# Joining the weights' sign bit on VectorE instead of ScalarE, and pooling the first keys on VectorE alone

## The chip, the core and the metric

The kernel runs on one core of a Trainium2 chip. The metric is device time in microseconds for one execution; the time before is the median of three runs. A profile of one further execution goes with it.

## What is computed

The program is pooled attention followed by a gated feed-forward layer, in float32 accuracy. There are 8 batches, 8 heads, 576 positions and a head size of 64, so 4608 tokens of width 512; the feed-forward layer is 1536 wide.

```python
k_p = k.reshape(B, H, Sp, 8, D).mean(axis=3)     # 72 pooled keys per batch and head
v_p = v.reshape(B, H, Sp, 8, D).mean(axis=3)
scores = scale * np.matmul(q, k_p.transpose(0, 1, 3, 2))
scores = scores - np.max(scores, axis=-1, keepdims=True)
attn = np.exp(scores)
attn = attn / (np.sum(attn, axis=-1, keepdims=True) + 1e-09)
x = np.matmul(attn, v_p)                         # then tokens x 512
g = x @ w_gate
silu = g * (1.0 / (1.0 + np.exp(-g)))
out = (silu * (x @ w_val)) @ w_out
```

The three weight matrices arrive as 64-bit floats. The kernel reads them as pairs of 32-bit words, a low and a high one, and builds a 32-bit float from each pair by integer operations and scaling.

## The kernel before

**Stages.** The 4608 tokens are cut into nine tiles of 512 columns. For each tile, attention makes x in chunks of at most 128 columns, and the feed-forward layer then runs over 12 weight blocks of 128 hidden columns. For accuracy nearly every operand is held as a high and a low part: x as xh and xl, the weights as wgv_h, wgv_l, wo_h and wo_l, the hidden activations as hh and hl. A block therefore needs 24 gate and value products (L423 to L425) and 12 output products (L407 to L409). The gate and value sums have one PSUM bank each; between the two groups of products stand a tanh (L427, ScalarE), two VectorE operations (L428, L431), a copy hh (L437, ScalarE) and a difference hl (L438, VectorE).

**The weights.** They stay in SBUF for the whole kernel and are converted once, while the first tile runs. Function `load_w` does one block of 128 x 1536 pairs: a load `ws` of 1.5 MB (L138); a shift of the low words by 29 (L141, VectorE); a write of the sign into the upper 16 bits of each low word (L143, ScalarE, a float16 output of the high word times 2^-60, of which only the sign remains); wf, the high word scaled without its sign (L146, ScalarE); the joining of wf and the low word (L148, VectorE). After that come the two maxima of the block (L155, ScalarE, each with a small read of its accumulator), the sum over partitions on TensorE and the power of two that scales the block (`pow2_above`, L126 to L133), the high parts (L168, ScalarE), the low parts (L169, VectorE), wo_h (L174, ScalarE) and wo_l (L175, GpSimd). Raw blocks share a pool of two buffers, `raw`; at the start one of the two holds the keys of batch 0. wf has one of three buffers of a pool `mid`, shared with keys, values and outputs.

**Keys and values.** `prep_k` loads a batch's keys in two halves (L199) and sums each group of 8 with `pool8`: on VectorE that is one reduction (L180), on GpSimd three additions of halves (L185 to L187). Before, VectorE does the first half of batch 0, and GpSimd everything else. Values go through the same three GpSimd additions, and then through a number of VectorE operations that split them (vst_h, vst_l, vst_f).

**A chunk of attention.** Eight small score products (L265), maxima and differences (L272, L273), an exponential (L281), sums and normalisation (L283 to L289), the weights as float16 halves (L295 and L297 on ScalarE, L298 and L299 on GpSimd), a transposing transfer issued by SyncE (L300), 16 products with the values (L309 to L312), then xh (L314, ScalarE) and xl (L315, VectorE).

**Order.** All engines work in order. The program is written as generators: before the first feed-forward step two chunks of attention are done, then each step takes four pieces of weight work (until the 12 blocks are done), one block of the feed-forward layer and three pieces of attention. The first tile runs its first three blocks in two halves of 256 columns. The framework then draws up each engine's order from estimated times and adds the waits, so the order of two independent instructions in the profile need not be that of the program.

Of the kernel before, what the change touches and what calls it, by code (L numbers as in the profile page):

```python
# [8 lines left out]
F16 = mybir.dt.float16  # L9
F32 = mybir.dt.float32  # L10
F32R = mybir.dt.float32r
U32 = mybir.dt.uint32
AF = mybir.ActivationFunctionType
ALU = mybir.AluOpType
# [30 lines left out]
def attention_then_swiglu(  # L45
# [9 lines left out]
    nc = tc.nc  # L55
# [3 lines left out]
    SP = S // POOLW  # L59
# [34 lines left out]
    for i in range(4):  # L94
# [3 lines left out]
        out=mask, in_=eye.rearrange("p (h k) -> p h k", h=4), axis=AX.X, op=ALU.add  # L98
# [23 lines left out]
    def pow2_above(dst, inv, src):  # L122

        ps = bank()
        sums = ps[:, : src.shape[1]]
        nc.tensor.matmul(sums, ones, src, start=True, stop=True)  # L126
        nc.vector.tensor_scalar(
            out=dst, in0=sums, scalar1=1e-30, scalar2=1.0 / UNIT, op0=ALU.max, op1=ALU.mult
        )
        nc.vector.tensor_single_scalar(  # L130
            dst.bitcast(U32), dst.bitcast(U32), 0x7F800000, ALU.bitwise_and
        )
        nc.vector.reciprocal(inv, dst)  # L133

    def load_w(c):

        ws = raw.tile([P, 3 * DM, 2], U32, name="ws", tag="raw")
        nc.sync.dma_start(out=ws, in_=w3[c].bitcast(U32))  # L138
        low, high = ws[:, :, 0], ws[:, :, 1]
        wf = mid.tile([P, 3 * DM], F32, name="wf", tag="mid")  # L140
        nc.vector.tensor_single_scalar(low, low, 29, ALU.logical_shift_right)  # L141

        nc.scalar.activation(  # L143
            ws.bitcast(F16)[:, :, 1], high.bitcast(F32), AF.Copy, scale=2.0**-60
        )
        nc.scalar.activation(wf, high.bitcast(F32), AF.Abs, scale=2.0**-112)  # L146
        yield
        nc.vector.scalar_tensor_tensor(  # L148
            out=wf.bitcast(U32), in0=wf.bitcast(U32), scalar=3, in1=low,
            op0=ALU.logical_shift_left, op1=ALU.bitwise_or,  # L150
        )
        wm = small.tile([P, 2], F32, name="wm")
        for i in range(2):
            part = wf[:, i * DM : (i + 1) * DM]
            nc.scalar.activation(  # L155
                wgv_h[:, c, i].rearrange("p j f -> p (j f)"), part, AF.Abs,
                accum_out=wm[:, i : i + 1],
            )
        yield
        sw = small.tile([P, 2], F32, name="sw")  # L160
        pow2_above(p2w[:, c, 0:2], sw, wm)
        nc.vector.tensor_mul(p2w[:, c, 2:3], p2w[:, c, 0:1], p2w[:, c, 1:2])
        yield
        for i in range(2):
            part = wf[:, i * DM : (i + 1) * DM]
            hi = wgv_h[:, c, i].rearrange("p j f -> p (j f)")
            lo = wgv_l[:, c, i].rearrange("p j f -> p (j f)")
            nc.scalar.activation(hi, part, AF.Copy, scale=sw[:, i : i + 1])  # L168
            nc.vector.scalar_tensor_tensor(  # L169
                out=lo, in0=part, scalar=sw[:, i : i + 1], in1=hi,  # L170
                op0=ALU.mult, op1=ALU.subtract
            )
        part = wf[:, 2 * DM :]
        nc.scalar.copy(wo_h[:, c, :], part)  # L174
        nc.gpsimd.tensor_sub(wo_l[:, c, :], part, wo_h[:, c, :].bitcast(F32))  # L175

    def pool8(eng, src, dst, inner):

        if eng is nc.vector:
            nc.vector.tensor_reduce(  # L180
                out=dst, in_=src.rearrange("p j (t i) -> p j i t", t=POOLW), axis=AX.X, op=ALU.add
            )
            return
        a, b4 = src[:, :, : 4 * inner], src[:, :, 4 * inner :]
        eng.tensor_add(a, a, b4)  # L185
        eng.tensor_add(a[:, :, : 2 * inner], a[:, :, : 2 * inner], a[:, :, 2 * inner :])
        eng.tensor_add(dst, a[:, :, :inner], a[:, :, inner : 2 * inner])  # L187

    def prep_k(b):
        ks = ksum[b % 2]  # L190
        for g in range(2):
            js = slice(g * NJ // 2, (g + 1) * NJ // 2)
            if b:
                kr = mid.tile([P, NJ // 2, S], F32, name="kr", tag="mid")
            else:
                if g == 0:
                    first = raw.tile([P, NJ, S], F32, name="k0", tag="raw")
                kr = first[:, js]
            nc.sync.dma_start(out=kr, in_=k[b, :, js])  # L199
            pool8(nc.gpsimd if b or g else nc.vector, kr, ks[:, js], SP)  # L200
            yield

    def prep_v(b):
# [118 lines left out]
    def prep(b):  # L322
        if b < B and b not in prepped:
            prepped.add(b)
            yield from prep_k(b)
            if b == 0:
                load_q(0, 0, SUB)
            yield from prep_v(b)
            yield
# [132 lines left out]
    def weights():  # L462
        for c in range(NCH):
            yield from load_w(c)
            ready.add(c)
# [112 lines left out]
```

## Time and profile before

| | |
|---|---|
| median of three runs | 1053.33 us (1053.12 to 1055.92) |
| the profiled execution | 1050.82 us, of which the span of the profile is 1049.0 us |
| TensorE busy | 991.8 us, 95% of the span |
| VectorE busy | 517.3 us, 49% |
| ScalarE busy | 332.7 us, 32% |
| GpSimd busy | 194.3 us, 19% |
| mean granted clock of TensorE | 0.993 |

The busy shares are averages over stages that differ: the weights are converted in the first fifth of the span, and the remaining tiles only use them. The rows below therefore go by stretches of time, counted from the start of the span. In them PE is TensorE, DVE VectorE, ACT ScalarE, POOL GpSimd and SPq SyncE's queue of transfers. A line number such as L143 is that of the kernel file.

### The profile page before, as it was taken

To read this page: it belongs to the slowest core of one execution; us is meant where nothing else is said; L and a number is where in the kernel's file an instruction comes from. 1 tells how busy PE (TensorE), PEld (TensorE's weight loads), DVE (VectorE), ACT (ScalarE), POOL (GpSimd) and SP (SyncE) were. 2 spreads that over 40 slices of the span, in tenths; PEclk is the share of its full clock that TensorE was granted. 3 is DMA by queue.
4 is the path that set the end of the run, shared out by engine and by line. 5 is a ranking of instruction groups with operands and counts; after the bars stand their busy time and mean duration, and the time that the engine had idled before them with its cause. 6 is when DMAs were issued, how large, how long until landed. Compare 5 with 4: busy or idle time off the path is not lost.

```text
span 1049.0 us, 13336 instructions
## 1 busy us (share of the span) xinstructions
PE 991.8 (95%) x5320; PEld 602.2 (57%) x5320; DVE 517.3 (49%) x1013; ACT 332.7 (32%) x549; POOL 194.3 (19%) x223
## 2 busy tenths in 40 slices
PE   3378989999999999999999999999999999999998
PEld 2256556665556655665566555655665556555555
DVE  6586878754246543644256435542553245223222
ACT  3897874332123312221133113311332132212111
POOL 5226136520006100610062005200110011000000
PEclk9998999999999999999999999999999999999999
DMA  7655435430032202410051006100210021001001
GB/s 283 203 178 185 155 90 151 159 67 13 1 111 80 52 1 73 129 31 1 35 161 41 7 5 187 46 1 0 77 40 16 1 75 27 1 1 41 1 1 41
DMA packets 81214, 72.43 MB, mean 69 GB/s; under 512 B 53504, under 2 KB 69888, under 8 KB 79616
## 3 DMA queue, kind: packets, MB, share of 16 engines
q1 hardware_dynamic: 81152, 71.58, 22.4%
q8 instruction: 42, 0.69, 0.3%
q14 instruction: 20, 0.16, 0.1%
HBM read 50.33 MB, written 9.44 MB: 57 GB/s over the span
## 4 chain that ended last, share of the span: by engine, by line
PE 84%; DVE 6%; ACT 4%; issue 3%; DMA 2%; POOL 1%; SPq 0%; ACTq 0%; POOLq 0%
PE gv L423 17%; PE gv L425 16%; PE gv L424 16%; PE acc L407 9%; PE acc L408 9%; PE acc L409 9%; PE ps L265 5%; ACT ws L143 2%; DVE wgv_l L169 1%; DVE wf L148 1%; PE ps L309 1%; DMA vr<-v_main 1%; DMA ws<-w_all 1%; PE ps L312 1%; PE ps L310 1%
## 5 line engine op out<-in xcount | busy, mean ns | idle before, releaser
L423 PE MATMUL gv<-xh,wgv_h 128*128 128x512 f16 (+1 forms) x888 | 334.6, 377 | 4.9 <-ACT xh L314 3.0
L425 PE MATMUL gv<-xh,wgv_l 128*128 128x512 f16 (+1 forms) x888 | 333.1, 376 | 1.5 <-DVE wgv_l L169 1.5
L424 PE MATMUL gv<-xl,wgv_h 128*128 128x512 f16 (+1 forms) x888 | 333.6, 376 | 0.0
L428 DVE SCALAR_TENSOR_TENSOR hf<-hf,gv 128x512 f32<-128x512 f32 (+1 forms) x111 | 74.3, 670 | 256.9 <-ACT hf L427 256.9
L407 PE MATMUL acc<-hh,wo_h 128*128 128x512 f32 (+1 forms) x444 | 184.0, 433 | 2.5 <-ACT hh L437 2.5
L408 PE MATMUL acc<-hl,wo_h 128*128 128x512 f32 (+1 forms) x444 | 172.5, 390 | 0.1
L409 PE MATMUL acc<-hh,wo_l 128*128 128x512 f32 (+1 forms) x444 | 171.8, 389 | 0.0
L427 ACT ACTIVATE hf<-gv,un 128x512 f32<-128x512 f32 (+1 forms) x111 | 74.7, 673 | 290.1 <-PE gv L425 290.1
L423 PEld LDWEIGHTS <-wgv_h 128*128 128x128 f16 x888 | 88.0, 99 | 110.5 <-issue 18.7
L425 PEld LDWEIGHTS <-wgv_l 128*128 128x128 f16 x888 | 87.6, 99 | 100.3 <-DVE wgv_l L169 1.8
L424 PEld LDWEIGHTS <-wgv_h 128*128 128x128 f16 x888 | 88.0, 99 | 86.2 <-issue 1.1
L437 ACT CAST hh<-hf 128x512 fp32r<-128x512 f32 (+1 forms) x111 | 67.6, 609 | 204.0 <-DVE hf L431 203.9
L431 DVE SCALAR_TENSOR_TENSOR hf<-gv,un,hf 128x512 f32<-128x512 f32 (+1 forms) x111 | 81.4, 734 | 82.6 <-PE gv L425 81.8
L298 POOL TENSOR_TENSOR half<-sc,half 128x512 f16<-128x512 f32 (+1 forms) x40 | 49.6, 1241 | 324.4 <-issue 244.7
L438 DVE TENSOR_TENSOR hl<-hf,hh 128x512 fp32r<-128x512 f32 (+1 forms) x111 | 81.0, 730 | 51.0 <-ACT hh L437 50.5
L407 PEld LDWEIGHTS acc<-hh,wo_h 128*128 128x128 f32 x444 | 82.5, 188 | 27.6 <-ACT hh L437 3.1
L409 PEld LDWEIGHTS acc<-hh,wo_l 128*128 128x128 f32 x444 | 83.8, 189 | 17.9
L408 PEld LDWEIGHTS acc<-hl,wo_h 128*128 128x128 f32 x444 | 84.1, 189 | 17.0 <-DVE hl L438 0.3
L265 PE MATMUL ps<-ksum,qt 64*128 64x72 f32 (+1 forms) x640 | 76.1, 286 | 11.8 <-DMA qt<-q_rows 8.9
L265 PEld LDWEIGHTS ps<-ksum,qt 64*128 64x128 f32 (+1 forms) x640 | 63.6, 190 | 38.6 <-issue 20.3
L185 POOL TENSOR_TENSOR kr<-kr 128x576 f32<-128x576 f32 x14 | 22.5, 1607 | 295.5 <-DMA kr<-k_rows 230.3
L309 PE MATMUL ps<-pt,vst_h 128*128 128x128 f16 (+1 forms) x160 | 33.8, 222 | 18.9 <-DMA pt<-half 18.0
(89 smaller groups left out, 833.8 us busy)
## 6 DMA issues: line engine op xcount, KB each, us to landing
ws<-w_all SPq DMA_DIRECT2D x12, 1536.0 KB, 6.9
out_t<-ob SPq DMA_DIRECT2D x36, 256.0 KB, 2.2
qt<-q_rows SPq DMA_DIRECT2D x32, 256.0 KB, 3.2
vr<-v_main SPq DMA_DIRECT2D x16, 512.0 KB, 3.9
kr<-k_rows SPq DMA_DIRECT2D x14, 576.0 KB, 4.4
vr<-v_left SPq DMA_DIRECT2D x8, 512.0 KB, 3.7
k<-k_rows SPq DMA_DIRECT2D x2, 576.0 KB, 4.3
qt<-q_rows SPq DMA_DIRECT2D x8, 128.0 KB, 2.6
```

The source lines that it names most:

```text
L265: nc.tensor.matmul(pss[g][:n, j * SP : (j + 1) * SP], qt[rows, j, :n], ksum[b % 2][rows, j, :], start=True, stop=True,)
L407: nc.tensor.matmul(o, wo_h[:, c, js], hh[:, :n], start=begin, stop=False)
L408: nc.tensor.matmul(o, wo_h[:, c, js], hl[:, :n], start=False, stop=False)
L409: nc.tensor.matmul(o, wo_l[:, c, js], hh[:, :n], start=False, stop=end)
L423: nc.tensor.matmul(o, wh, xh[:, j, a:e], start=(j == 0), stop=False)
L424: nc.tensor.matmul(o, wh, xl[:, j, a:e], start=False, stop=False)
L425: nc.tensor.matmul(o, wl, xh[:, j, a:e], start=False, stop=(j == NJ - 1))
L427: nc.scalar.activation(hf[:, :n], pss[0], AF.Tanh, scale=un[:, c, 0:1])
L428: nc.vector.scalar_tensor_tensor(out=hf[:, :n], in0=hf[:, :n], scalar=1.0, in1=pss[0], op0=ALU.add, op1=ALU.mult)
L431: nc.vector.scalar_tensor_tensor(out=hf[:, :n], in0=pss[1], scalar=un[:, c, 2:3], in1=hf[:, :n], op0=ALU.mult, op1=ALU.mult,)
L437: nc.scalar.copy(hh[:, :n], hf[:, :n])
L438: nc.vector.tensor_sub(hl[:, :n], hf[:, :n], hh[:, :n].bitcast(F32))
```

## The change

The ScalarE write of the sign is replaced by a VectorE operation that takes the sign bit from the high words and joins it to the low words, in 32-bit words and in place. It stands between the shift and the scaling in the program. In `prep_k`, both halves of batch 0's keys go to VectorE; later batches stay on GpSimd.

```diff
         nc.vector.tensor_single_scalar(low, low, 29, ALU.logical_shift_right)
-
-        nc.scalar.activation(
-            ws.bitcast(F16)[:, :, 1], high.bitcast(F32), AF.Copy, scale=2.0**-60
+        nc.vector.scalar_tensor_tensor(
+            out=low, in0=high, scalar=0x80000000, in1=low, op0=ALU.bitwise_and, op1=ALU.bitwise_or
         )
         nc.scalar.activation(wf, high.bitcast(F32), AF.Abs, scale=2.0**-112)
...
             nc.sync.dma_start(out=kr, in_=k[b, :, js])
-            pool8(nc.gpsimd if b or g else nc.vector, kr, ks[:, js], SP)
+            pool8(nc.gpsimd if b else nc.vector, kr, ks[:, js], SP)
```

## Rows read from the trace of the kernel before

**Rows 1.** Busy time by stretch; x is instructions, PEclk the mean granted clock.

```profile
core 0: us, PE busy (x) PEld busy (x) DVE busy (x) ACT busy (x) POOL busy (x), PEclk, DMA share, GB/s
20.00:55.00 35.00, 11.59 (x66) 9.37 (x66) 22.12 (x53) 30.79 (x32) 8.62 (x7) 1.00 0.55 171
55.00:120.00 65.00, 54.02 (x362) 39.49 (x361) 51.45 (x105) 53.06 (x76) 27.44 (x25) 0.92 0.60 207
...
58.00:70.00 12.00, 8.98 (x69) 7.47 (x67) 10.77 (x24) 10.68 (x23) 4.21 (x5) 0.86 0.84 280
...
120.00:190.00 70.00, 65.03 (x385) 40.04 (x384) 55.14 (x106) 43.36 (x73) 27.92 (x28) 0.98 0.33 94
20.00:190.00 170.00, 130.64 (x810) 88.90 (x810) 128.71 (x263) 127.21 (x179) 63.98 (x60) 0.96 0.48 153
190.00:1049.00 859.00, 854.13 (x4471) 507.56 (x4470) 375.95 (x723) 202.23 (x366) 116.61 (x137) 1.00 0.16 46
```

**Rows 2.** Waits up to 55 us: total us, times, longest us.

```profile
PE ps L309 <- DMA pt<-half: 11.4, 2, 9.7
PE ps L126 <- DVE xl L315: 3.2, 1, 3.2
...
DVE wf L148 <- ACT ws L143: 6.6, 3, 5.0
```

**Rows 3.** TensorE's waits from 55 to 190 us, same columns.

```profile
PE ps L309 <- DMA pt<-half: 6.6, 3, 3.5
PE gv L423 <- ACT xh L314: 3.0, 1, 3.0
PE acc L407 <- ACT hh L437: 2.5, 2, 2.0
...
PE gv L423 <- DVE hf L431: 0.4, 1, 0.4
```

**Rows 4.** Instructions of single lines: ns min/median/max, first and last start.

```profile
L143 ACT ACTIVATE ws<-ws x12: 3581/3637/3699, 21.6 to 143.6; 128x1536 f16<-128x1536 f32 x12
...
L146 ACT ACTIVATE wf<-ws x12: 1576/1618/1699, 19.5 to 147.5; 128x1536 f32<-128x1536 f32 x12
...
L141 DVE TENSOR_SCALAR ws<-ws x12: 944/950/1252, 20.1 to 142.5; 128x1536 uint32<-128x1536 uint32 x12
...
L148 DVE SCALAR_TENSOR_TENSOR wf<-wf,ws x12: 1741/1758/2089, 25.2 to 149.4; 128x1536 uint32<-128x1536 uint32 x12
...
L180 DVE TENSOR_REDUCE ksum<-k x1: 2218/2218/2218, 5.8 to 5.8; 128x144 f32<-128x1152 f32 x1
```

**Rows 5.** Timeline of ScalarE, three places: start us, us, instruction.

```profile
28.77 3.62 ACT L143 ACTIVATE ws<-ws 128x1536 f16<-128x1536 f32 x1
...
32.14 0.67 ACT L295 CAST half<-sc 128x512 f16<-128x512 f32 x1
...
44.60 3.60 ACT L143 ACTIVATE ws<-ws 128x1536 f16<-128x1536 f32 x1
47.96 0.67 ACT L314 ACTIVATE xh<-ps,r 128x512 f16<-128x512 f32 x1
...
50.73 3.62 ACT L143 ACTIVATE ws<-ws 128x1536 f16<-128x1536 f32 x1 [0.17 <-DVE p2w L127]
54.10 2.50 ACT L168 ACTIVATE wgv_h<-wf,sw 128x512 f16<-128x512 f32 x4
```

**Rows 6.** L143 alone on ScalarE, by stretch.

```profile
20.00:55.00 35.00, 18.01 (x5) 1.00 0.55 171
55.00:190.00 135.00, 25.58 (x7) 0.95 0.46 149
```

**Rows 7.** Timeline around the first scores; in brackets the idle time before.

```profile
11.79 0.49 POOL L187 TENSOR_TENSOR ksum<-k 128x144 f32<-128x144 f32 x1
...
12.33 1.13 PE L265 MATMUL ps<-ksum,qt 64*128 64x72 f32 x8 [2.68 <-POOL ksum L187]
...
13.49 0.82 DVE L272 TENSOR_REDUCE mx<-ps 128x4 f32<-128x288 f32 x2 [5.46 <-PE ps L265]
```

## The prediction

> **What bounds the kernel now.** I read the busy times by stretch first. From 190 us to the end TensorE is busy for 854.13 of 859 us, so nothing that ends there can shorten the kernel by more than 5 us [rows 1]. Between 20 and 190 us it is busy for 130.64 of 170: 39.4 us are idle there. The weights are converted in that stretch, and the change touches only that stretch and the first microseconds, so every gain or loss is made before 190 us. In the same row VectorE is busy for 128.71 us and ScalarE for 127.21: two engines share the conversion, and neither is far ahead. Up to 120 us ScalarE is the fuller of the two (30.79 against 22.12 of 35 us, then 53.06 against 51.45 of 65), after that VectorE (55.14 against 43.36 of 70).
>
> Next I read what TensorE waits for. Between 20 and 55 us it waits longest for the transposed weights of the attention (11.4 us) and once for the low half of x (3.2) [rows 2]. After 55 us the longest waits are the same transfer (6.6), x's high half (3.0) and the copy of h (2.5) [rows 3]. All of these come out of ScalarE or pass through it, and the timeline says why they are late: half L295 starts at 32.14, xh L314 at 47.96 and wgv_h L168 at 54.10, each as the next instruction behind an L143 write that began about 3.4 us before [rows 5]. TensorE's first gate product follows that L168. L143 takes 3.64 us; L146 reads the same high words, as many of them, in 1.62 [rows 4]. Twelve L143 make 43.59 us of ScalarE's 127.21 [rows 1, 6].
>
> **The change part by part.**
>
> *Taken away:* the twelve L143, 5 before 55 us and 7 after it, 18.01 and 25.58 us [rows 6]. ScalarE falls to 127.2 - 43.6 = 83.6 us of 170. L148 no longer waits for ScalarE's write, which before 55 us kept VectorE idle for 6.6 us in three places [rows 2].
>
> *Added:* twelve VectorE operations with two sources in SBUF, 1536 words of 32 bits, sources and output at a step of two words. None stands in the trace. From below, L141 reads and writes those same stepped words with one source in 0.95 us; from above, L143, which writes into the same words from ScalarE, takes 3.64. Between them L148, the same kind of operation with two sources, one of them stepped, takes 1.76 (1.74 to 2.09) [rows 4]. I take 1.76: only more of its operands are stepped, and L141 shows no price for the step. That is 21.1 us (11.4 to 43.7), and VectorE's load in the stretch becomes 128.7 + 21.1 = 149.8 us.
>
> *Two sources beside GpSimd:* the spread of L148, 1.76 to 2.09, is small [rows 4]. The Trainium skill ("SBUF — State Buffer", section "SBUF: two separate sides") says that a VectorE operation with two SBUF inputs and a GpSimd operation that reads SBUF hold a port pair exclusively, the later one waiting. The trace agrees in that GpSimd was busy for 63.98 us of the stretch and the slowest L148 took 0.33 us more than the median [rows 1, 4]. If all twelve were stretched so, VectorE would get another 4 us; the sum here has none of it.
>
> *First keys:* the second half of batch 0's keys went through three GpSimd additions, of which the last starts at 11.79 and takes 0.49; the first scores' second half starts at 12.33 behind it [rows 7]. On VectorE the reduction takes 2.22 us, like that of the first half, which started at 5.8 [rows 4]: it can run from 8.0 to 10.3, in the 5.46 us that VectorE stood idle before L272 [rows 7]. So TensorE may go on 2.0 us earlier, and the buffer that the keys share with the raw weights comes free as much earlier, so that SyncE can issue the second weight load sooner. What stands against a full gain is that the attention's next inputs and the first weights are transfers that don't depend on it. Between 0 and 2.0 I take 1.0. If VectorE's idle time weren't there, the reduction's 2.2 us would delay L272 instead.
>
> *20 to 55 us:* three instructions on the way to the first gate product stand directly behind an L143, with at most 32.14 - 28.77 = 3.4, 47.96 - 44.60 = 3.4 and 54.10 - 50.73 = 3.4 us to gain, 10.1 in all [rows 5]. Their own inputs come while the write runs, so not all of it: I take two thirds, 6.7. VectorE pays 5 x 1.76 = 8.8 us and gets the 6.6 us of waiting back, so 2.2 more stay on its queue, in front of the attention's operations. Net 4.5 us earlier (bounds: 10.1 earlier to 8.8 - 6.7 = 2.1 later).
>
> *55 to 190 us:* of TensorE's waits I put x's high half (3.0), h's copy (2.5) and half of the transposed weights' (3.3) down to ScalarE's queue: 8.8 us, which is 34% of the 25.58 us of L143 there [rows 3, 6]. If VectorE's new operations reach TensorE at the same rate, 7 x 1.76 x 0.34 = 4.2 us come back. Net 4.6 earlier (bounds: 8.8 earlier to 12.3 - 8.8 = 3.5 later).
>
> *The loads:* a raw buffer is loaded anew when L148 has read it. With L148 earlier SyncE issues the next load earlier, and GpSimd's wo_l and the transposes behind it move along; this only moves transfers that share the stretch already, and I give it nothing.
>
> The sum is 1.0 + 4.5 + 4.6 = 10.1 us. But it must fit on VectorE: 149.8 us of work in 170 - 9.1 = 160.9 us would be 93%. The fullest long stretch of VectorE in this trace is 58 to 70 us, 10.77 of 12, or 90% [rows 1]. At 90% the stretch takes 166.4 us, 3.6 less than now, with the keys 4.6. Between 4.6 and 10.1 I take 6, nearer to the cap, since the engine that gets the work is by then the fullest. The profiled run took 1050.8 us around a span of 1049.0, and lies 2.5 under the median of the runs, 1053.3. So I forecast a span of 1043.0, a run of 1044.8 and a median of 1047.3.
>
> **The rivals.**
>
> *The whole sum comes, and more.* VectorE could put off what isn't urgent until after 190 us, where it was busy for 375.95 of 859 us [rows 1]. Then the 10.1 us come whole, 1043.2. Fewer pauses would also raise the clock: 55 to 120 us had a mean granted clock of 0.92, so 16% of 65 us at 1.2 in place of 2.4 GHz, worth at most 5.2 us. Together down to 1038.
>
> *VectorE takes ScalarE's place as the bound, and nothing is left.* At the share that ScalarE had where it was fullest for long, 30.79 of 35 us or 88% [rows 1], VectorE's 149.8 us need 170 us: the same as now, and with the keys 1052.3. The Trainium skill ("Perfetto Trace Analysis", section "Identifying the Most-Contended Engine") says that the engine with the highest occupancy is the one to relieve. By that rule moving work to VectorE, the busier of the two in 20 to 190 us, gives nothing. The trace bears it out only in part: the occupancies differ by 1.5 us, and TensorE's waits name ScalarE far more often than VectorE, whose entry for hf is 0.4 us [rows 1 to 3].
>
> *Slower: the weights' operations stand in front of h's.* VectorE works in order, and the gate and value banks are single: TensorE can't start the next block before L431 has read them. Today that wait is 0.4 us [rows 3]; with three operations of 1 to 1.8 us in a row for each weight block it can grow, and VectorE then idles in turn for TensorE. The point from which this decides is the share that VectorE reaches: 88% is no change; at 84% the stretch takes 178.3 us, 8.3 longer, about 1060.6 with the keys. Its own average now is 128.71 of 170, 76% [rows 1], which speaks for this; that it reached 90% with such a mix from 58 to 70 us speaks against.
>
> *The change isn't cheap.* If the stepped output costs as much as L143's, VectorE gets 43.7 us, 172.4 in all, and at 90% the stretch takes 191.6: 21.6 longer, about 1074. L141's 0.95 us speaks against it.
>
> **How the numbers follow.** Chances: forecast (3.2 to about 9.5 us faster) 0.43; the whole sum and more 0.14; no change left 0.23; slower by h's chain 0.17; a dear operation 0.03. This kernel's measurement tells about 0.3%, 3.2 us, from no change. So faster 0.57, same 0.23, slower 0.20. For 8 in 10 the range runs from 1040 to 1057: it leaves out half of the first rival, the upper half of the third and the last, 0.07 + 0.09 + 0.03.
>
> **What would show it.** In the profile of the changed kernel: no L143 on ScalarE, whose busy time in 20 to 190 us is near 84 us; twelve new VectorE operations of about 1.76 us; VectorE the fullest engine of that stretch at about 90%; the first L168 near 48 us in place of 54.1; the second key reduction on VectorE from 8.0 to 10.3. TensorE's waits for xh and hh shrink, and those for hf, xl, wgv_l and vst grow from under 2 us each to a few. The forecast is wrong if the new operation takes over 2.2 us, if VectorE idles between weight operations for the next load (then transfers, not engines, set the pace), or if the earlier start is given back before 120 us by waits for VectorE. With the instructions' order drawn up anew for the changed work, the attention's operations can also change places with the weights', by some microseconds either way.

## The result and the profile after

The changed kernel takes 1057.53 us (median of 17 runs, 1056.26 to 1062.61), the kernel before 1054.52 us (17 runs, 1052.65 to 1058.06). The ratio is 1.0033, with a 95% interval of 1.0020 to 1.0046: slower by about 3.5 us, where 1047.3 had been forecast. The profiled execution took 1056.66 us around a span of 1054.9, 5.9 more than the span before, which is of an execution 3.7 us under its median (this one lies 0.9 under). All ratios compare executions in the chip's usual state; the profile of keys_only fell in its slow one and is not read.

Line numbers after L142 are one lower than before: L145 is the scaling of wf, L147 its joining, L167 and L168 the high and low parts, L422 to L424 the gate and value products, L426 the tanh, L427 and L430 the two VectorE operations on h, L436 and L437 hh and hl.

Busy time by stretch of the kernel after, with the columns of [rows 1]:

```profile
core 0: us, PE busy (x) PEld busy (x) DVE busy (x) ACT busy (x) POOL busy (x), PEclk, DMA share, GB/s
...
20.00:55.00 35.00, 13.35 (x72) 10.35 (x72) 30.95 (x53) 13.50 (x26) 9.01 (x5) 1.00 0.59 173
55.00:120.00 65.00, 50.93 (x359) 37.07 (x357) 56.63 (x99) 37.93 (x72) 27.73 (x25) 1.00 0.63 204
58.00:70.00 12.00, 7.12 (x61) 5.65 (x59) 11.93 (x15) 9.57 (x24) 7.12 (x6) 1.00 0.91 249
120.00:190.00 70.00, 63.59 (x363) 39.09 (x361) 61.47 (x124) 35.31 (x67) 27.51 (x28) 0.98 0.33 95
20.00:190.00 170.00, 127.87 (x789) 86.51 (x788) 149.05 (x274) 86.74 (x165) 64.25 (x58) 0.99 0.50 153
```

The work moved as forecast: ScalarE has 86.74 us in 20 to 190 where it had 127.21, VectorE 149.05 where it had 128.71. VectorE is now nearly full for longer than any row of before showed: 88% up to 55 us, 11.93 of 12 us from 58 to 70, 88% from 120 to 190. TensorE's count of products says where it was lost: from 20 to 120 us TensorE did 431 of them (428 before), and from 120 to 190 only 363 (385 before).

TensorE lost 2.8 us of busy time in 20 to 190 (127.87 against 130.64), and 2.8 us more at two later places, where before it never stood idle (busy for 10.00 of 10 us and 200.00 of 200 in the same two stretches):

```profile
190.00:200.00 10.00, 8.73 (x50) 6.24 (x51) 6.82 (x27) 1.65 (x3) 0.00 (x0) 0.83 0.42 136
...
400.00:600.00 200.00, 198.47 (x1077) 118.53 (x1076) 96.82 (x195) 49.92 (x93) 41.31 (x48) 1.00 0.22 63
```

Its total is the same, 992.0 us against 991.8. So nearly all of the 5.9 us is idle time of TensorE; the products don't take longer. The last 1.5 us of it, between 400 and 600 us, lie where no weights are converted and VectorE is half idle, so a full VectorE doesn't explain them.

What the engines waited for from 20 to 55 us (total, times, longest), against [rows 2]:

```profile
PE ps L308 <- DMA pt<-half: 8.1, 1, 8.1
...
PE ps L310 <- DVE vst_l L223: 3.8, 1, 3.8
PE ps L308 <- DVE vst_h L222: 3.7, 1, 3.7
...
PE ps L311 <- DVE vst_f L236: 2.8, 1, 2.8
PE acc L515 <- DVE p2v L130: 2.7, 1, 2.7
...
PE ps L126 <- DVE p2w L127: 0.3, 1, 0.3
...
PE gv L424 <- DVE wgv_l L168: 0.2, 1, 0.2
```

VectorE no longer waits for ScalarE's write, and TensorE's wait for the transposed weights is shorter (8.1 us, 11.4 before), but behind it TensorE waits for the values that VectorE splits, 10.3 us in three places. It did so before as well, for 6.0 us in two. These are the entries of TensorE before, in the same stretch, that [rows 2] doesn't have:

```profile
PE ps L311 <- DVE vst_l L224: 3.8, 1, 3.8
...
PE ps L312 <- DVE vst_f L237: 2.2, 1, 2.2
PE acc L516 <- DVE p2v L130: 1.4, 1, 1.4
PE acc L516 <- DVE sc L273: 1.4, 1, 1.4
PE gv L423 <- ACT wgv_h L168: 1.2, 1, 1.2
PE ps L265 <- DVE p2w L127: 0.2, 1, 0.2
```

From 55 to 190 us, TensorE alone, against [rows 3]:

```profile
PE gv L422 <- DVE hf L427: 9.5, 4, 3.5
PE ps L264 <- DVE p2w L127: 3.9, 2, 2.0
PE acc L407 <- DVE hl L437: 3.6, 3, 2.4
PE ps L264 <- DVE sc L272: 0.7, 1, 0.7
PE gv L422 <- ACT wgv_h L167: 0.7, 2, 0.4
PE ps L308 <- DMA pt<-half: 0.4, 2, 0.2
```

The entries of before that [rows 3] doesn't have:

```profile
PE gv L425 <- DVE wgv_l L169: 1.5, 1, 1.5
PE gv L423 <- ACT wgv_h L168: 1.2, 1, 1.2
PE ps L309 <- DVE sc L273: 0.9, 1, 0.9
PE ps L126 <- ACT wgv_h L155: 0.6, 1, 0.6
...
PE gv L423 <- DVE hf L428: 0.3, 1, 0.3
```

The waits for ScalarE's xh and hh (5.5 us before) have gone from the list, and of the transfer's 6.6 us 0.4 are left. VectorE stands there in their place, with 17 us in three entries. That is the picture of the rival "the weights' operations stand in front of h's". Added up from 20 to 190 us, TensorE's waits for ScalarE and for the transfer fell from 26.5 to 9.2 us, and those for VectorE rose from 15.3 to 31.2.

The lines that answer to [rows 4]: ns min/median/max, first and last start.

```profile
L142 DVE SCALAR_TENSOR_TENSOR ws<-ws x12: 1741/1752/2703, 21.1 to 144.4; 128x1536 uint32<-128x1536 uint32 x12
...
L145 ACT ACTIVATE wf<-ws x12: 1597/1625/1705, 18.2 to 151.3; 128x1536 f32<-128x1536 f32 x12
...
L147 DVE SCALAR_TENSOR_TENSOR wf<-wf,ws x12: 1744/1752/2041, 23.8 to 152.9; 128x1536 uint32<-128x1536 uint32 x12
...
L179 DVE TENSOR_REDUCE ksum<-k x2: 2197/2202/2207, 5.8 to 7.9; 128x144 f32<-128x1152 f32 x2
```

The new operation costs what was put down for it. How a VectorE queue that is full delays a block is seen on ScalarE and VectorE around the ninth feed-forward step, which is the sixth weight block, since the first three were done in halves. On ScalarE:

```profile
116.80 0.68 ACT L426 ACTIVATE hf<-gv,un 128x512 f32<-128x512 f32 x1
...
127.15 0.61 ACT L436 CAST hh<-hf 128x512 fp32r<-128x512 f32 x1
...
133.86 0.69 ACT L426 ACTIVATE hf<-gv,un 128x512 f32<-128x512 f32 x1
```

On VectorE, in the same stretch:

```profile
118.49 0.14 DVE L127 TENSOR_SCALAR p2w<-ps 128x2 f32<-128x2 f32 x1
118.55 1.75 DVE L142 SCALAR_TENSOR_TENSOR ws<-ws 128x1536 uint32<-128x1536 uint32 x1
...
122.77 0.16 DVE L130 TENSOR_SCALAR p2w<-p2w 128x2 uint32<-128x2 uint32 x1
...
122.96 0.68 DVE L427 SCALAR_TENSOR_TENSOR hf<-hf,gv 128x512 f32<-128x512 f32 x1
...
125.73 0.15 DVE L133 RECIPROCAL sw<-p2w 128x2 f32<-128x2 f32 x1
...
125.94 0.73 DVE L430 SCALAR_TENSOR_TENSOR hf<-gv,un,hf 128x512 f32<-128x512 f32 x1
```

No row here has a bracket: VectorE was never idle. The ninth tanh came at 116.80, 5.9 us ahead of before (122.67). Its next operation L427 ran 5.5 us after the tanh had ended, and hh began 10.4 us after the tanh began (7.8 before). The three small operations L127, L130, L133 that find a block's scale take 0.45 us together and were spread over 7.4 us (121.72 to 124.64, 2.9 us, before). The tenth tanh then came at 133.86, 1.3 us later than before (132.52). The lead was had, and it was gone within one block.

### The profile page after: what moved, and what is told of

It reads as the page before. It is cut to its first block, busy times and chain, and to the rows that moved or that the text cites. A ratio compares the mean times of both kernels' runs of the same rounds, so it can differ in the third digit from the quotient of the medians.

```text
span 1054.9 us, 13329 instructions
## 1 busy us (share of the span) xinstructions
PE 992.0 (94%) x5320; PEld 602.3 (57%) x5320; DVE 540.0 (51%) x1026; ACT 293.6 (28%) x537; POOL 192.9 (18%) x220
## 4 chain that ended last, share of the span: by engine, by line
PE 78%; DVE 9%; DMA 5%; POOL 4%; issue 2%; ACT 1%; SPq 0%; POOLq 0%; ACTq 0%; DVEq 0%
PE gv L422 16%; PE gv L424 15%; PE gv L423 15%; PE acc L406 8%; PE acc L407 8%; PE acc L408 8%; PE ps L264 5%; POOL vr L184 2%; DMA vr<-v_main 2%; DMA ws<-w_all 1%; DVE wgv_l L168 1%; DVE wf L147 1%; DVE ws L142 1%; DVE hl L437 1%; POOL vr L185 1%
## 5 line engine op out<-in xcount | busy, mean ns | idle before, releaser
L422 PE MATMUL gv<-xh,wgv_h 128*128 128x512 f16 (+1 forms) x888 | 334.0, 376 | 10.2 <-DVE hf L427 9.5
L424 PE MATMUL gv<-xh,wgv_l 128*128 128x512 f16 (+1 forms) x888 | 331.8, 375 | 0.2 <-DVE wgv_l L168 0.2
L427 DVE SCALAR_TENSOR_TENSOR hf<-hf,gv 128x512 f32<-128x512 f32 (+1 forms) x111 | 74.4, 670 | 252.0 <-ACT hf L426 251.9
L426 ACT ACTIVATE hf<-gv,un 128x512 f32<-128x512 f32 (+1 forms) x111 | 74.8, 673 | 291.8 <-PE gv L424 291.7
L422 PEld LDWEIGHTS <-wgv_h 128*128 128x128 f16 x888 | 87.6, 99 | 105.1 <-issue 15.5
L424 PEld LDWEIGHTS <-wgv_l 128*128 128x128 f16 x888 | 87.3, 98 | 99.6 <-DVE wgv_l L168 1.1
L423 PEld LDWEIGHTS <-wgv_h 128*128 128x128 f16 x888 | 87.4, 98 | 95.7 <-issue 10.4
L436 ACT CAST hh<-hf 128x512 fp32r<-128x512 f32 (+1 forms) x111 | 67.5, 608 | 215.9 <-DVE hf L430 215.9
L430 DVE SCALAR_TENSOR_TENSOR hf<-gv,un,hf 128x512 f32<-128x512 f32 (+1 forms) x111 | 81.5, 734 | 82.5 <-PE gv L424 81.7
L297 POOL TENSOR_TENSOR half<-sc,half 128x512 f16<-128x512 f32 (+1 forms) x40 | 50.2, 1254 | 325.2 <-issue 244.0
L437 DVE TENSOR_TENSOR hl<-hf,hh 128x512 fp32r<-128x512 f32 (+1 forms) x111 | 82.9, 747 | 49.5 <-ACT hh L436 49.2
L406 PEld LDWEIGHTS acc<-hh,wo_h 128*128 128x128 f32 x444 | 83.4, 191 | 25.4 <-ACT hh L436 0.7
L407 PEld LDWEIGHTS acc<-hl,wo_h 128*128 128x128 f32 x444 | 84.0, 189 | 21.1 <-DVE hl L437 4.5
```

Of the source, the lines that this page charges most:

```text
L406: nc.tensor.matmul(o, wo_h[:, c, js], hh[:, :n], start=begin, stop=False)
L407: nc.tensor.matmul(o, wo_h[:, c, js], hl[:, :n], start=False, stop=False)
L422: nc.tensor.matmul(o, wh, xh[:, j, a:e], start=(j == 0), stop=False)
L423: nc.tensor.matmul(o, wh, xl[:, j, a:e], start=False, stop=False)
L424: nc.tensor.matmul(o, wl, xh[:, j, a:e], start=False, stop=(j == NJ - 1))
L426: nc.scalar.activation(hf[:, :n], pss[0], AF.Tanh, scale=un[:, c, 0:1])
```

## Experiments

The records below name theories by letters. The first theory: VectorE is full from about 100 us on, so the late blocks' new operations carry the loss. Its rivals: K, the keys; O, the redrawn order of all engines; S, the same price on either engine; M, the early lead is lost at the pool `mid`; E, the total of work; G, ScalarE's writes were covered by other work. Added later: L, short VectorE operations that free PSUM banks wait behind long ones; W, VectorE's amount of work; C, the step that is added to each block's chain.

One caution for all of them. Two small edits of the kernel before, a fourth buffer and a small copy, made it 4.7 and 3.9 us slower (below). Each edit has its order of instructions drawn up anew, so I don't read a difference of 3 or 4 us between two versions as a mechanism; one of 15 us I do. The change's own 3.5 us is of that small size too.

The profiled executions, one of each version, show where its time lies. All do the same 5320 products; idle is the span without TensorE's busy time, in us, and the last column is TensorE's mean granted clock over the execution.

| | span | TensorE busy | idle | clock |
|---|---|---|---|---|
| before | 1049.0 | 991.8 | 57.2 | 0.993 |
| after | 1054.9 | 992.0 | 62.9 | 0.995 |
| twice | 1063.5 | 1000.0 | 63.5 | 0.987 |
| mid4_before | 1058.7 | 998.8 | 59.9 | 0.987 |
| scalar_sums_before | 1058.6 | 1001.5 | 57.1 | 0.985 |
| no_sign | 1035.5 | 987.7 | 47.8 | 0.997 |
| beside | 1050.1 | 994.1 | 56.0 | 0.993 |

The two small edits of before lost their time mostly in longer products at a lower granted clock (7.0 of 9.7 us in mid4_before, all of the 9.6 in scalar_sums_before), not in idle time. So the clock differs from version to version, as the order does, and no run separates the two.

### The two parts alone

`sign_only`: the kernel before with the new operation.

```diff
-            pool8(nc.gpsimd if b else nc.vector, kr, ks[:, js], SP)
+            pool8(nc.gpsimd if b or g else nc.vector, kr, ks[:, js], SP)
```

> The sign on VectorE for all 12 blocks, the keys as before. Theory (VectorE is full between about 100 and 150 us, and the new operations cost there what they won earlier): the whole loss is here, 2 to 5 us slower than before, VectorE near 147 us busy from 20 to 190 us. Rival K (the keys' reduction on VectorE is what costs): no slower than before, or up to 3 us faster. Rival O (only the redrawn order of instructions decides): anywhere within 4 us of before.

Measured: 1.0023 (1.0008 to 1.0038), 1055.35 us.

`keys_only`: the kernel before with the keys on VectorE.

```diff
-            pool8(nc.gpsimd if b or g else nc.vector, kr, ks[:, js], SP)
+            pool8(nc.gpsimd if b else nc.vector, kr, ks[:, js], SP)
```

> Both halves of the first keys on VectorE, the sign on ScalarE as before. Theory: within 1.5 us of before; the second half of the first scores starts near 10.3 us instead of 12.3, and that is lost again in the waits for the first weights. Rival K: 3 us slower or more. Rival O: anywhere within 4 us of before.

Measured: 1.0006 (0.9994 to 1.0019), 1054.66 us. The sign alone makes the kernel slower by 0.23% where the full change has 0.33%, with overlapping intervals; the keys cost nothing that can be measured, and K falls. They give nothing either, though the second reduction ran where it was expected (the two from 5.8 to 10.1, by the row of L179 above).

### Early and late blocks

`early_vector`: the full change for the first six blocks, ScalarE's write for the others; `late_vector`: the reverse; `split8`: as the first, with eight blocks. The edit of the first:

```diff
-        nc.vector.scalar_tensor_tensor(
-            out=low, in0=high, scalar=0x80000000, in1=low, op0=ALU.bitwise_and, op1=ALU.bitwise_or
-        )
+        if c < 6:
+            nc.vector.scalar_tensor_tensor(
+                out=low, in0=high, scalar=0x80000000, in1=low, op0=ALU.bitwise_and, op1=ALU.bitwise_or
+            )
+        else:
+            nc.scalar.activation(
+                ws.bitcast(F16)[:, :, 1], high.bitcast(F32), AF.Copy, scale=2.0**-60
+            )
```

> The keys on VectorE, the sign on VectorE for blocks 0 to 5 (those converted up to about 90 us) and on ScalarE for blocks 6 to 11. Theory: the early gain stays and the late loss goes, 3 to 7 us faster than before. Rival K: slower than before by about 3 us, as the full change. Rival O: within 4 us of before, with no order between this run and the next.

> The keys on VectorE, the sign on ScalarE for blocks 0 to 5 and on VectorE for blocks 6 to 11. Theory: no early gain, but the late loss, 3 to 9 us slower than before and slower than the full change. Rival K: about 3 us slower, as the full change. Rival O: within 4 us of before, with no order between this run and the one before it.

> As the run with the sign of blocks 0 to 5 on VectorE, but with blocks 0 to 7 there and only 8 to 11 on ScalarE. In the full change blocks 6 and 7 have their sign joined at 75 and 90 us, before VectorE is full; on ScalarE these two writes stand in front of x's high half and h's copy. Theory (VectorE has no room from 100 to 150 us, ScalarE has): the lead of the full change at the ninth step (116.8 us against 122.7) is kept in part, 1 to 5 us faster than before. Rival S (a block's sign costs about the same on either engine wherever it stands): between before and the full change, 0 to 3 us slower.

Measured: early_vector 1.0005 (0.9990 to 1.0021), late_vector 1.0029 (1.0015 to 1.0043), split8 1.0006 (0.9992 to 1.0019). The busy times from 100 to 150 us of split8 and of the kernel after, where the last blocks are converted:

```profile
100.00:150.00 50.00, 45.20 (x237) 26.38 (x235) 40.30 (x83) 42.48 (x59) 14.36 (x12) 0.93 0.43 151
```

```profile
100.00:150.00 50.00, 43.68 (x236) 27.49 (x235) 47.15 (x88) 28.31 (x54) 14.63 (x12) 0.97 0.45 153
```

With the late writes on ScalarE VectorE has 40.30 of 50 us there, else 47.15. The six early blocks on VectorE cost nothing net, the late ones about 3 us, which is what the first theory says; but the 3 to 7 us and 1 to 5 us that it gave to early_vector and split8 over the kernel before did not come, and late_vector isn't slower than the full change. Early on, what the one engine gets back the other pays, which is S's reading, and O can't be excluded at this size.

### Twice the dose, and a fourth buffer

`twice`: the full change with the new operation written twice for each block (the second one changes nothing).

```diff
+        nc.vector.scalar_tensor_tensor(
+            out=low, in0=high, scalar=0x80000000, in1=low, op0=ALU.bitwise_and, op1=ALU.bitwise_or
+        )
```

> The full change with the new VectorE operation done twice in each block (the second changes nothing), 21 us more work on VectorE. Theory: VectorE is the bound of the stretch, so at 88% of its time the stretch grows by 12 us or more against the full change, about 1069, most of it after 100 us. Rival S: the operation costs about as little again as the change itself, 2 to 4 us against the full change. Rival O (only the redrawn order of instructions decides): within 4 us of the full change, either way.

Measured: 1.0093 (1.0077 to 1.0110), 1064.73 us. Another 21 us on VectorE cost 1.0093 - 1.0033 = 0.60%, 6.3 us. That is half of what the theory put down (12 or more) and over what S and O did (up to 4). VectorE took the work into its pauses; it was busy for 95% of the stretch, so the 88% that the theory went by was no limit:

```profile
20.00:190.00 170.00, 125.84 (x733) 85.46 (x734) 161.63 (x276) 83.00 (x157) 60.73 (x46) 0.93 0.47 148
```

By the table TensorE's idle time hardly rose against the full change (63.5 us against 62.9); its products took 8.0 us longer, at a granted clock of 0.93 in this stretch against 0.99.

`mid4` and `mid4_before`: the full change, and the kernel before, with a fourth buffer in the pool of wf.

```diff
-    mid = ctx.enter_context(tc.tile_pool(name="mid", bufs=3))
+    mid = ctx.enter_context(tc.tile_pool(name="mid", bufs=4))
```

> The full change with four buffers instead of three in the pool that the scaled weights share with keys, values and outputs. In before and after alike no block is joined between 80 and 100 us, while batch 1's keys and values hold that pool. Theory M (the early lead is lost there: the weights stand still and come in one burst after 100 us, when VectorE is full): block 6 is joined well before 100 us, and the time falls by 3 us or more against the full change. Rival E (the engine's total work alone decides): within 1.5 us of the full change.

> The kernel before with four buffers instead of three in the same pool. Theory M: gains less than the full change does with the fourth buffer, since ScalarE is the fuller engine up to 100 us and joins no earlier; 0 to 2 us. Rival E: within 1.5 us of before.

Measured: mid4 1.0006 (0.9994 to 1.0017), 1055.17 us; mid4_before 1.0045 (1.0028 to 1.0063), 1059.69 us. In the kernel after, VectorE sat idle for 3.9 us behind a late L145 and then did two blocks' joinings in a row:

```profile
99.92 3.44 DVE L147 SCALAR_TENSOR_TENSOR wf<-wf,ws 128x1536 uint32<-128x1536 uint32 x2 [3.93 <-ACT wf L145]
```

With the fourth buffer the same pair runs about 7.5 us earlier:

```profile
92.41 4.14 DVE L147 SCALAR_TENSOR_TENSOR wf<-wf,ws 128x1536 uint32<-128x1536 uint32 x2
```

The change then costs nothing that can be measured, which agrees with M. But the same buffer makes the kernel before 4.7 us slower, which no theory had; by the table most of that lies in longer products, and its cause is open. As both are of the size of a redrawn order, M is not shown.

### No sign at all, and the same work off the chain

`no_sign`: the keys on VectorE, and the sign joined on no engine; it leaves the weights' signs out.

```diff
-        nc.vector.scalar_tensor_tensor(
-            out=low, in0=high, scalar=0x80000000, in1=low, op0=ALU.bitwise_and, op1=ALU.bitwise_or
-        )
```

> The sign is joined nowhere: ScalarE's writes are gone and VectorE gets nothing (this leaves the weights' signs out). Keys on VectorE. Theory (taking ScalarE's 43.6 us away gains some 3 us, adding VectorE's 21.1 us costs some 6, as the second dose did): 2 to 5 us faster than before. Rival G (ScalarE's writes were covered by other waits and gain nothing): within 1 us of the run with only the keys moved. The forecast made before the result: about 9 us faster.

Measured: 0.9858 (0.9840 to 0.9876), 1038.87 us, that is 15.0 us faster than before. So ScalarE's twelve writes were not covered (G falls): taking them away is worth about the 16.5 us that the forecast's sum has for it (the 2 to 5 us of the theory, and its 9, were too small), and VectorE's twelve operations cost 1.0033 - 0.9858 = 1.75%, 18.4 us for 23.1 us of work.

`beside`: no_sign with a VectorE operation of the same size behind the joining of each block. It reads wf and writes a tile that nobody reads. VectorE gets the work, but no block waits for its result; the signs are left out here too.

```diff
+    aside = const.tile([P, 3 * DM], U32, name="aside")
...
+        nc.vector.scalar_tensor_tensor(
+            out=aside, in0=wf.bitcast(U32), scalar=3, in1=wf.bitcast(U32),
+            op0=ALU.logical_shift_left, op1=ALU.bitwise_or,
+        )
```

> The sign joined nowhere (the weights' signs are left out), and in its place a VectorE operation of the same kind and size behind each block's joining, which reads wf and writes a tile that nobody reads: the same 21 us of VectorE, but no block waits for it. Rival W (VectorE's amount of work): as slow as the full change, within 4 us of 1057. Rival C (the step that the operation adds to each block's chain): 1040 to 1047. If weights without signs were what made the run without the sign fast, this one would be near 1039 as well.

Measured: 1.0001 (0.9989 to 1.0013), 1053.36 us. The busy times of no_sign:

```profile
100.00:150.00 50.00, 50.00 (x296) 31.00 (x294) 46.86 (x104) 30.66 (x61) 14.95 (x15) 1.00 0.38 118
...
20.00:190.00 170.00, 139.44 (x880) 94.54 (x881) 137.85 (x297) 89.99 (x171) 62.60 (x60) 0.99 0.54 170
```

And of beside:

```profile
100.00:150.00 50.00, 46.39 (x256) 29.25 (x255) 47.93 (x92) 25.85 (x47) 18.58 (x11) 1.00 0.38 128
...
20.00:190.00 170.00, 131.84 (x799) 90.19 (x797) 147.95 (x273) 87.06 (x165) 72.59 (x58) 0.96 0.48 153
```

This is the run that decides. Work that nothing waits for takes 1.43%, 15.0 us, and puts TensorE back from 880 products to 799 by 190 us, against 810 before. It is VectorE's amount of work (W) that eats the gain: ScalarE is as free in both (89.99 and 87.06 us). W's forecast came, within 4 us of 1057; C's 1040 to 1047 did not. Not all of the loss is waiting: of the 14.6 us between the two spans 8.2 are idle time of TensorE, and 6.4 lie in its products, whose granted clock was 0.96 in the stretch and 0.99 in no_sign. It also shows that the weights without signs are not what made no_sign fast. VectorE is as full from 100 to 150 us in both (46.86 and 47.93), but in no_sign it does 104 instructions in that time, in beside 92, of which some are the added ones. Between beside and the full change 0.32%, 3.4 us, are left, for the step in the chain (C) or a different order; that is of the size of an order, and not told apart.

### Shorter pieces, and VectorE relieved of a PSUM read

`thirds`: the new operation in three pieces of 512 words.

```diff
-            out=low, in0=high, scalar=0x80000000, in1=low, op0=ALU.bitwise_and, op1=ALU.bitwise_or
-        )
+        for i in range(3):
+            third = slice(i * DM, (i + 1) * DM)
+            nc.vector.scalar_tensor_tensor(
+                out=low[:, third], in0=high[:, third], scalar=0x80000000, in1=low[:, third],
+                op0=ALU.bitwise_and, op1=ALU.bitwise_or,
+            )
```

> The full change with the new operation cut into three of 512 words each. Theory L (what costs is the time that VectorE's short operations, which hand back the two shared PSUM banks and the gate banks, stand behind one of 1.75 us): 1 to 4 us faster than the full change. Rival W (VectorE's amount of work): 0 to 2 us slower than the full change, since each piece has its own fixed time, some 2 us more in all.

Measured: 1.0063 (1.0048 to 1.0077), 1060.07 us. `scalar_sums` and `scalar_sums_before`: ScalarE copies the sums of `pow2_above` out of PSUM, in the full change and in the kernel before, so that the bank is free without VectorE.

```diff
+        got = small.tile([P, 2], F32, name="got")[:, : src.shape[1]]
+        nc.scalar.copy(got, sums)
...
-            out=dst, in0=sums, scalar1=1e-30, scalar2=1.0 / UNIT, op0=ALU.max, op1=ALU.mult
+            out=dst, in0=got, scalar1=1e-30, scalar2=1.0 / UNIT, op0=ALU.max, op1=ALU.mult
```

> The full change, and ScalarE, which now has room, copies the sums of pow2_above out of PSUM, so that the bank goes back to TensorE without VectorE. Theory L: TensorE's waits for p2w (3.9 us after 55 us) vanish, and the time falls by 2 to 4 us against the full change. Rival W: no gain, or up to 1 us slower, since VectorE's work is the same and each chain has one step more.

> The kernel before with the same copy by ScalarE. Theory L: gains less than with the full change, or loses, since here the copy stands behind ScalarE's 3.6 us writes: 0 to 4 us slower than before. Rival W: within 1 us of before.

Measured: scalar_sums 1.0037 (1.0024 to 1.0050), scalar_sums_before 1.0037 (1.0022 to 1.0051). In the full change TensorE's waits for p2w, which the copy was to remove, are gone from its list after 55 us, and the time hasn't fallen; the pieces, which take 25.4 us in all and not 23.1, make it 3.2 us slower where W had up to 2. So nothing speaks for L in the full change. In the kernel before the copy costs 3.9 us, which L had and W had not; by the table it lies in longer products, not in waits. Differences of this size don't decide between the two.

### The sign by other means

`halfwords`: one source instead of two, on VectorE, writing only the upper half of each low word.

```diff
-        nc.vector.scalar_tensor_tensor(
-            out=low, in0=high, scalar=0x80000000, in1=low, op0=ALU.bitwise_and, op1=ALU.bitwise_or
-        )
+        ws16 = ws.bitcast(mybir.dt.uint16)
+        nc.vector.tensor_single_scalar(ws16[:, :, 1], ws16[:, :, 3], 0x8000, ALU.bitwise_and)
```

> The sign taken as 16-bit words: one VectorE operation with one source writes the upper half of each low word from the upper half of the high word, masked. If it costs what L141 costs (0.95 us, one source, the same step), VectorE gets 11.4 us instead of 21.1, and both rivals W and C expect 5 to 10 us less than the full change, 1047 to 1052. If writing 16 bits at a step of 8 bytes costs on VectorE what it costs on ScalarE (3.6 us), VectorE gets 43 us and the time is 1064 or more.

Measured: 1.0042 (1.0028 to 1.0056), 1057.50 us. The row of its line shows that it is no cheaper than what it replaces:

```profile
L143 DVE TENSOR_SCALAR ws<-ws x12: 1808/1880/2553, 20.8 to 143.1; 128x1536 uint16<-128x1536 uint16 x12
```

Neither of the two expected prices (0.95 and 3.6 us) came. It is as much work on VectorE as the full change has (23.7 us, 23.1 there), and the same time: that agrees with W.

`gpsimd_sign`: ScalarE's float16 write done by GpSimd.

```diff
-        nc.vector.scalar_tensor_tensor(
-            out=low, in0=high, scalar=0x80000000, in1=low, op0=ALU.bitwise_and, op1=ALU.bitwise_or
-        )
+        nc.gpsimd.tensor_scalar_mul(ws.bitcast(F16)[:, :, 1], high.bitcast(F32), 2.0**-60)
```

> The float16 write of before, done by GpSimd instead of ScalarE; keys on VectorE. GpSimd was busy for 64 of 170 us. Rival W: VectorE and ScalarE are both relieved, so near the run without the sign plus some waiting for the port that both share, 1040 to 1048. Rival C: a GpSimd operation of 1536 elements takes 3 us or more in each block's chain, so 1050 or more.

Measured: 1.0430 (1.0407 to 1.0454), 1098.96 us. Its new line:

```profile
L142 POOL TENSOR_SCALAR ws<-ws x12: 6134/6228/7668, 20.1 to 190.4; 128x1536 f16<-128x1536 f32 x12
```

And its groups of VectorE instructions up to 190 us (busy us, mean ns of one, idle before):

```profile
L145 DVE SCALAR_TENSOR_TENSOR wf<-wf,ws 128x1536 uint32<-128x1536 uint32 x10 | 27.4, 2752 | 0.8 <-ACT wf L143 0.8
...
L234 DVE TENSOR_SCALAR vst_f<-fh,mask 128x128 f16<-128x128 f16 x8 | 14.1, 2196 | 0.0
```

GpSimd had room by its busy time (63.98 of 170 us, [rows 1]), but each write takes 6.2 us, and VectorE gets slower beside it: by their means the joining takes 2752 ns where the kernel after has 1778, and a small masking operation 2196 where it has 242. The median of the masking is 248 ns in both kernels; its mean comes from a few, the longest of 6.20 us, about as long as one GpSimd write. So C's 1050 or more came and W's 1040 to 1048 did not, but neither had put down that VectorE's other operations get slower too.

## Why the prediction was wrong

*ScalarE's side: right in size, in part by luck.* The gain put down for it was 1.0 + 6.7 + 8.8 = 16.5 us; without the sign on any engine the kernel is 15.0 us faster. But the 16.5 were all to be waiting time of TensorE, and in no_sign its idle time fell by 9.4 us; another 4.1 came from shorter products at a higher clock (0.99 against 0.96), which only a rival had, and the keys' 1.0 didn't come. The three places behind L143 cleared too: the first L167 starts at 50.89 where L168 had started at 54.10 (48 was forecast), TensorE's waits for xh and hh are gone, and those for the transposed weights are 8.5 us where they were 18.0.

*The price of the operation: right.* 1.752 us against 1.76. The twelve took 23.1 us and not 21.1, as a few were stretched, to 2.70 at most. That is 2 us of the 4 that the two-source paragraph had left out of the sum. The Trainium skill's rule of the exclusive port pair ("SBUF — State Buffer", section "SBUF: two separate sides") agrees with where the longest one lies: it started at 36.03, while GpSimd's L174 and L297 ran without a gap from 35.76 to 39.74.

*VectorE's price for the end: the step that failed.* The forecast charged VectorE 2.2 us up to 55 us, since it got 6.6 us of waiting back, and 4.2 us after, "at the same rate" of 34% at which ScalarE's writes had shown in TensorE's waits: 6.4 us in all, and 10.5 with the cap of 90%. The runs put it at 18.4 us, of which 15.0 come from the amount alone. The refund before 55 us was real (VectorE's idle time there fell from 12.88 to 4.05 us, and TensorE did 72 products instead of 66), but it was a loan: VectorE was busy for 87 to 88% from there on, and the lead of 3 to 6 us was gone by the tenth tanh. And a rate read from ScalarE's writes, on an engine with 25% of its time free, was carried over to one that was about to have 12% left. VectorE's own waits had not been added up. By the lists of before, TensorE waited for VectorE 10 times and 15.3 us from 20 to 190 us, for ScalarE 6 times and 8.5 us; that it names ScalarE "far more often" is a wrong reading, and so is that the waits for xl and vst were "under 2 us each" (3.2, and 3.8 and 2.2). A microsecond of work on VectorE cost 0.66 us off the chain (15.0 for beside's 22.6) and 0.80 in it (18.4 for 23.1), not 0.34; a second one cost 0.29 (6.3 for 21.4), so that no single rate holds.

*The cap.* "90%" was taken from the fullest twelve microseconds. VectorE reached 87 to 88% over three long stretches, the share of the rival "nothing is left", but the time came out 3.5 us above before where that rival had 1.0 below. Neither share is a limit, since twice reached 95%. Nor is the work of the 170 us fixed: no_sign, without the sign on any engine, has VectorE busy there for 137.85 us, 9 more than before, since more other work falls into it. That the change's 149.05 us met the forecast's 149.8 is so in part chance; by 190 us it had done 21 products fewer than before. And 2.8 us were lost after 190 us, where the forecast had seen nothing to gain or lose. The rival "slower" had the mechanism, h's chain and the small scale operations behind the weights' long ones, and the mark that was named for it, the wait for hf that grows (from 0.7 us in its two entries to 9.5). Those for xl and wgv_l, which were to grow as well, did not. Its size was too large: 84% and 1060.6 us. The waits show that mechanism in the trace; that it, and not another delay of a full VectorE, is the whole loss was not shown.

*By the skill's rule.* The Trainium skill ("Perfetto Trace Analysis", section "Identifying the Most-Contended Engine") says to relieve the engine with the highest occupancy. VectorE led by only 1.5 us [rows 1], and the forecast counted the names in TensorE's waits for more. In this case the change is no gain, as the rule has it. But taking work off ScalarE alone gave 15.0 us in no_sign although VectorE led, and no run took work off VectorE, so the rule itself isn't tested here.

*The keys: right in what happens, wrong by 1 us in what it is worth.* keys_only is not distinguishable from before.

*The clock* rose as the first rival had it, from 0.92 to 1.00 in 55 to 120 us, and fell to 0.83 in 190 to 200 us, behind a stretch in which TensorE had been idle for 1.6 of 10 us. TensorE needed 50.93 us for 359 products from 55 to 120 where 54.02 had gone into 362, but the waits for VectorE took that back. The table shows that other versions have other clocks, so this part can't be counted on.

*Open:* why a second dose of 21 us costs 6.3 us where the first costs 15 to 18 (the traces show that VectorE still had pauses, and that the loss lies in longer products at a lower clock); why a fourth buffer helps the full change and harms the kernel before; and whether the last 3.4 us are the chain's step or the order.

## What to carry to other kernels

When two engines share a stretch at nearly the same load, price moved work by the waits for the engine that receives it, and not at the rate at which the giver's waits show; add up the whole list of waits by engine first. Here 43.6 us off ScalarE gave 15 us, and 23 us onto VectorE took 18, though 21 us more took only 6: the full duration is the careful bound, not a rule. Ask of any refunded wait what the receiving engine has put off meanwhile, and look for the point at which that comes due. To price an engine's amount of work by itself, add an operation of the same size whose result nobody reads, and see whether the time it costs is idle time or a lower clock.

## What the runs showed of the hardware

Operations on 16-bit values at a step of 8 bytes were dear here. ScalarE took 3.64 us to write 1536 of them and 1.62 us to write 1536 32-bit values side by side [rows 4]. VectorE's 16-bit operation with one source, which also read at that step, took 1.88 us, its 32-bit one on the same stepped words 0.95 [rows 4], so that half the bits cost twice the time, and no less than the two-source operation on whole words (1.75). GpSimd took 6.23 us for the write; no run has it write 32-bit values there. Beside it a masking operation of VectorE, 0.25 us by its median, took up to 6.20.
